# Sliding-window attention and a three-way maxout feed-forward on one core: the scores of tiles 6, 12 and 18 as one unit

## The chip, the cores and the metric

The kernel runs on one core of a Trainium2 chip. The core has five instruction streams that run side by side and wait for each other by semaphores: TensorE (PE in the profile; its weight loads are listed apart as PEld), VectorE (DVE), ScalarE (ACT), GpSimd (POOL) and SyncE (SP), which here only issues DMAs. Matrix products are written to PSUM, which the program treats as eight banks of 512 float32 for each of 128 partitions. The metric is the time on the device in microseconds (us) for one launch; a lower time is better. In the profile, "the span" runs from the first to the last instruction, so the time of a run is a little longer than its span.

## The reference

Four batches of eight heads, 768 positions, head width 64. Each position attends to the 96 latest positions including itself and to the first eight positions of its sequence, with a bias that falls linearly with distance at a slope of its own for each head. The result, 3072 rows of 512, goes through a feed-forward layer with three weight matrices, whose elementwise maximum is projected back to 512.

```python
scores = scale * np.matmul(q, k.transpose(0, 1, 3, 2))
is_global = pos[None, :] < int(n_global)            # n_global = 8
is_local = (rel >= 0) & (rel < int(n_local))        # n_local = 96
bias = -slopes[:, None, None] * dist[None, :, :]
a = softmax(where(keep, scores + bias, -1e9)); attn = a @ v
x = attn.transpose(0, 2, 1, 3).reshape(B * S, H * D)
h = np.maximum(np.maximum(x @ w1, x @ w2), x @ w3)  # 512 -> 768
out = h @ w_out                                     # 768 -> 512
```

## The kernel before, in words

**Tiles.** The 3072 rows are 24 tiles of 128 positions. Six tiles make a batch, so tiles 0, 6, 12 and 18 begin a batch. Because the window is 96 long, a tile's queries need only the keys of the tile itself and of the tile before it; the eight global keys and values are copied into rows of the tile before (units G and V). A tile that begins a batch has no tile before it, and so half the scores of any other tile.

**A schedule written out by hand.** The string SCHEDULE holds 782 short codes. Each code calls one function, which issues the instructions of one piece of work, and the order of the codes is the order of the instructions on every engine; nothing reorders them afterwards. A code such as S7.1.0@2 reads: unit S, tile 7, group 1, variant 0, buffer slot 2. Slots are assigned by hand too: "@" gives the PSUM bank or the place in a ring of SBUF buffers, and a unit that takes a bank has to wait until the bank's last reader is done. Units S and A take two neighbouring banks, units F, O, t and x one bank.

**The units that matter here.**

- l, c, x, y, X: load q and k, cast them to bf16 (c), and bring them into transposed form, either by TensorE (x, line 274) and a copy (y, line 285), or by one DMA transpose on SP's queue (X, line 290).
- S (line 347): the scores of a tile for four heads (group 0 or 1), eight small matmuls for an ordinary tile, four for a tile that begins a batch. The pairs of heads alternate between the two banks of the unit. The result is 128 partitions by 4 heads by 2 key tiles by 128 queries; in a tile that begins a batch only one of the two key places is filled.
- e (line 354): the exponential on ScalarE, from PSUM to a buffer P in SBUF; 1024 elements per partition for an ordinary tile, 512 for a tile that begins a batch.
- m (lines 363 and 365): the product of P with the mask and bias factors (wmask), on VectorE; line 363 for ordinary tiles, 365 for tiles that begin a batch.
- A (lines 389 and 392): probabilities times values, with a column of ones in the values for the sum; 16 matmuls for an ordinary tile, 8 for a tile that begins a batch, into two banks.
- n (lines 400 and 401): reciprocal of the sum and scaling, from PSUM to xb on VectorE; t, u (lines 416 and 419) or Z (line 422, DMA) transpose xb into xT for the feed-forward.
- F (line 431): one 128-row block of one of the three products of a chunk of 2 or 4 tiles, four matmuls into one bank. f evicts it: the first of the three by a cast to h01 (line 445, on ScalarE with variant 0, on VectorE with variant 1), the second by a maximum with h01 (447), the third by a maximum into ht (450).
- O (line 455) and o (line 469): the output projection of one tile, six matmuls into one bank, and its copy to the staging buffer, on ScalarE (variant 0) or VectorE (variant 1). s sends it out.
- G and V (lines 313 and 323): the copies of global keys and values.

**Where the change sits.** Three stretches: around tile 6 (about 45 to 56 us in the profile), where tile 8's transposes x4 and y4 and the feed-forward blocks F1.4 and F1.5 share the banks with S6, S7, A6 and A7; around tile 12 (about 64 to 72 us); and around tile 18 (about 90 to 100 us), whose keys and queries come by the DMA transpose X18. TensorE takes its instructions strictly in the order of the schedule, so a unit that waits holds everything behind it.

Of the kernel before, what the change touches and what calls it, by code (L numbers as in the profile page):

```python
# [55 lines left out]
    F3.0.0@1 f3.4.0.0@4 f3.0.0.1@0 m13.0.1 v13.1.1 f2.4.2.1 F3.1.0@4 F3.3.0@5 c0.9.2.0@2 f3.3.0.0@1 c1.7.2.0
    A12@2 n12@1 f2.3.2.1 f3.1.0.1@2 F3.1.1@1 f3.1.1.1 v13.0.1 l1.9.2@0 c1.9.2.0 F3.0.2@0 F3.0.1@5 f3.0.1.1
    F3.1.2@4 f3.0.2.1@1 F3.2.0@1 F3.2.2@2 f3.1.2.1 F3.5.0@3 A13@4 V13.1.1 f3.5.0.1@3 n13@0 l2.9.2@2 l0.8.2@5
    c0.8.2.2@0 v19.0.2 V13.0.0 f3.2.0.0@0 v14.0.2 F3.5.1@0 F3.2.1@6 f3.2.1.1 f3.2.2.1 F3.3.1@1 F3.5.2@3 v18.1.0
    X14@3 v14.1.2 X15 f3.5.1.1 f3.3.1.1 F3.4.1@2 c1.8.2.0 S14.0.0@4 S14.1.0@0 e14.0@6 G14.2 f3.4.1.1 F3.4.2@6  # L60
# [4 lines left out]
    G16.0 Z14 o3.1.0@11 m16.0.1 V15.0.1 S17.0.0@0 Z12 S19.0.0@2 Z15 l2.8.2@1 e19.0@7 S17.1.0@4 e17.1@0 m17.1.1  # L65
    F4.4.0@6 e17.0@5 l0.11.2@1 s1.0 l2.10.2@0 F4.2.0@7 l1.10.2@2 F4.1.0@2 F4.5.0@3 v16.0.0 v16.1.0 F4.3.0@0
    A16@4 f4.2.0.0@2 Z18@2 V16.1.2 V16.0.2 f4.3.0.0@0 G18.0 F4.1.2@1 f4.1.0.1@3 m17.0.1 v17.0.1 v17.1.1
    l2.11.2@2 n16@3 s3.1 f4.5.0.0@4 m19.0.1 l0.10.2@3 F4.0.1@0 F4.1.1@7 m19.1.1 f4.4.0.0@1 F4.5.2@6 A19@2
    V19.0.2 v20.0.2 c0.11.2.2@1 c0.10.2.2@2 Z16 n19@1 Z19 G19.0 s0.1 s2.1 f4.1.1.1 f4.1.2.1@0 V19.1.1 F4.0.0@4
    F4.4.1@5 A17@2 c1.10.2.0 f4.0.0.1@3 n17@2 F4.5.1@7 f4.5.1.1 F4.2.1@1 F4.3.2@4 f4.5.2.1 f4.4.1.1 F4.0.2@2  # L70
# [25 lines left out]
def kernel(  # L96
# [239 lines left out]
    def u_S(slot, T, g, how):  # L336
        n = 2 if T % NT else 1
        biased[T, g] = how
        if not how:
            sps[T, g] = ring("sp", slot, [128, 2, 2, 2, 128], FP32, "sp")  # L340
        sp = sps[T, g]
        for ds in range(n):
            for j2 in range(2):
                jp = 2 * g + j2
                for hh in range(2):
                    hsl = slice(64 * hh, 64 * hh + 64)
                    nc.tensor.matmul(sp[:, hh, j2, ds], qT(T - ds, 1, hsl, jp), qT(T, 0, hsl, jp),  # L347
                                     start=not how, stop=True, skip_group_check=True)
# [8 lines left out]
    def u_m(slot, T, g, how):  # L357
# [4 lines left out]
        if T % NT:  # L362
# [15 lines left out]
    def u_A(slot, T):  # L378
# [3 lines left out]
        for g in range(2):  # L382
            P = Pt[T, g]
            for j2 in range(2):
                for hh in range(2):
# [3 lines left out]
                    nc.tensor.matmul(o, P[:, i, 0], heads(va(T))[:, h], start=True, stop=(t == 0),  # L389
# [220 lines left out]
```

## Time and profile before

| What | Value |
|---|---|
| Time, median of 3 runs (lowest to highest) | 175.57 us (175.31 to 175.96) |
| Time of the profiled execution | 175.37 us |
| Its span | 173.6 us |
| TensorE busy | 165.8 us, 95% of the span |
| VectorE busy | 130.5 us, 75% |
| ScalarE busy | 97.5 us, 56% |
| GpSimd busy | 52.7 us, 30% |
| Granted TensorE clock | 1.00 |

The profile's page gives busy times by engine and by group of instructions, and the chain of work that ended last: starting from the last instruction, it goes back at each step to whatever released that instruction, or to the one before it on its engine. The window table gives busy time by stretch, and the timeline lists instructions in order of time, with the idle time ahead of them in brackets and what ended it. In a timeline row the second number is the time from the start of the first to the end of the last instruction that is merged into the row; neighbouring matmuls overlap, so the chain, which counts each piece from the end of the one before, is the better view of how long a run of matmuls took.

### The profile page before, as it was taken

What the parts mean: (1) busy time and instruction counts of PE and PEld (TensorE: products, weight loads), DVE (VectorE), ACT (ScalarE), POOL (GpSimd) and SP (SyncE); (2) the same over time, 40 slices, a digit from 0 to 9 for tenths busy, and PEclk for the clock granted to TensorE, in tenths of its full rate; (3) what the DMA queues carried; (4) which work ended last, traced back from release to release, by engine and by line L of the source; (5) the groups of instructions that cost most, each with busy time, mean ns of one, the idle gap of its engine ahead of it and who ended that gap; (6) DMA issues with size and microseconds to landing.
All of it is one profiled execution on the core that took longest, in us unless ns stands there. A gap on an engine that the chain in (4) does not pass through costs nothing.

```text
span 173.6 us, 3857 instructions
## 1 busy us (share of the span) xinstructions
PE 165.8 (95%) x1485; PEld 93.7 (54%) x1507; DVE 130.5 (75%) x267; ACT 97.5 (56%) x149; POOL 52.7 (30%) x97
## 2 busy tenths in 40 slices
PE   7998999999999999999999999999999999999992
PEld 2455745567676767744445545544445654444442
DVE  7889884988699799798798479599578994064910
ACT  5988896771876878653657689200345551502032
POOL 4049396059498315200630001440530000000000
PEclk9999999999999999999999999999999999999999
DMA  5999999999999899699978799999990044380026
GB/s 135 359 294 324 401 362 384 291 364 315 291 292 189 130 263 166 175 299 289 148 129 138 72 212 312 309 228 265 262 203 29 0 125 119 124 302 0 2 73 233
DMA packets 66259, 37.36 MB, mean 215 GB/s; under 512 B 24128, under 2 KB 61120, under 8 KB 66240
## 3 DMA queue, kind: packets, MB, share of 16 engines
q1 hardware_dynamic: 66096, 37.04, 84.6%
q8 instruction: 12, 0.20, 0.5%
q10 hardware_dynamic: 144, 0.07, 0.1%
q14 instruction: 7, 0.06, 0.1%
HBM read 25.17 MB, written 6.29 MB: 181 GB/s over the span
## 4 chain that ended last, share of the span: by engine, by line
PE 85%; DVE 5%; DMA 3%; ACT 3%; issue 2%; SPq 0%; DVEq 0%
PE psum L431 51%; PE psum L455 18%; PE psum L347 6%; PE psum L389 3%; DMA rawqk<-in_k_dram 3%; PE psum L392 3%; PE psum L274 2%; ACT P L354 1%; PE psum L268 1%; PE psum L333 1%; PE psum L416 1%; DVE xb L401 1%; ACT xT L419 1%; ACT qb L193 1%; DVE P L365 0%
## 5 line engine op out<-in xcount | busy, mean ns | idle before, releaser
L431 PE MATMUL psum<-xT,w 128*128 128x512 bf16 (+1 forms) x491 | 97.4, 348 | 1.3 <-DVE ht L450 0.3
L431 PEld LDWEIGHTS <-w 128*128 128x128 bf16 x504 | 47.7, 98 | 42.4 <-issue 0.7
L354 ACT ACTIVATE P<-psum 128x1024 bf16<-128x1024 f32 (+1 forms) x48 | 43.3, 955 | 10.6 <-PE psum L347 10.5
L447 DVE TENSOR_TENSOR h<-h,psum 128x512 bf16<-128x512 bf16 (+1 forms) x42 | 25.1, 606 | 16.0 <-PE psum L431 12.1
L455 PE MATMUL psum<-wo,ht 128*128 128x512 bf16 (+2 forms) x147 | 33.5, 362 | 0.5
L445 ACT CAST h<-psum 128x512 bf16<-128x512 f32 (+1 forms) x27 | 13.9, 525 | 31.0 <-PE psum L431 27.8
L450 DVE TENSOR_TENSOR ht<-h,psum 128x512 bf16<-128x512 bf16 (+1 forms) x42 | 26.2, 643 | 2.1 <-PE psum L431 1.0
L363 DVE TENSOR_TENSOR P<-P,wmask 128x1024 bf16<-128x1024 bf16 x34 | 24.6, 738 | 1.6 <-ACT P L354 1.5
L455 PEld LDWEIGHTS <-ht 128*128 128x128 bf16 x156 | 13.9, 98 | 13.5
L252 POOL CAST va<-rawv 64x512 bf16<-64x512 f32 x28 | 18.4, 662 | 4.0 <-DMA rawv<-in_v_dram 2.9
L321 POOL COPY va<-vaf 4x260 int32<-4x260 int32 x17 | 6.8, 400 | 40.9 <-PE psum L392 40.5
L401 DVE TENSOR_TENSOR xb<-psum,rz 128x512 bf16<-128x512 f32 x24 | 16.6, 692 | 0.8
L469 ACT COPY staging<-psum 128x512 f32<-128x512 f32 x14 | 8.2, 592 | 12.8 <-PE psum L455 12.8
L347 PE MATMUL psum<-qkT 64*128 64x128 bf16 x352 | 14.5, 217 | 0.7 <-DVE qkT L313 0.4
L347 PEld LDWEIGHTS <-qkT 64*128 64x128 bf16 x352 | 10.1, 94 | 8.2 <-issue 6.2
L389 PEld LDWEIGHTS <-P 128*128 128x128 bf16 x192 | 12.6, 97 | 3.2 <-ACT P L354 0.4
L199 POOL CAST qb<-rawq 128x512 bf16<-128x512 f32 x14 | 9.1, 678 | 16.6 <-DMA rawq<-in_q_dram 16.4
L389 PE MATMUL psum<-va,P 128*128 128x65 bf16 x160 | 12.6, 193 | 0.1
L445 DVE CAST h<-psum 128x512 bf16<-128x512 f32 (+1 forms) x15 | 9.1, 614 | 4.0 <-PE psum L431 3.9
L392 PEld LDWEIGHTS <-P 128*128 128x128 bf16 x160 | 10.4, 97 | 1.5 <-DVE va L323 0.3
L199 POOL CAST qb<-rawk 128x512 bf16<-128x512 f32 x10 | 6.4, 677 | 12.5 <-DMA rawk<-in_k_dram 12.3
L392 PE MATMUL psum<-va,P 128*128 128x65 bf16 x128 | 9.9, 193 | 0.0
(72 smaller groups left out, 121.1 us busy)
## 6 DMA issues: line engine op xcount, KB each, us to landing
rawv<-in_v_dram SPq DMA_DIRECT2D x12, 512.0 KB, 7.1
out_dram<-staging SPq DMA_DIRECT2D x22, 256.0 KB, 2.5
rawq<-in_q_dram SPq DMA_DIRECT2D x10, 512.0 KB, 7.0
rawk<-in_k_dram SPq DMA_DIRECT2D x10, 512.0 KB, 7.4
staging<-in_moe_w_dram SPq DMA_DIRECT2D x3, 1024.0 KB, 9.3
staging<-in_moe_w_dram SPq DMA_DIRECT2D x3, 512.0 KB, 8.8
staging<-in_moe_w_out_dram SPq DMA_DIRECT2D x3, 512.0 KB, 6.4
rawqq<-in_q_dram SPq DMA_DIRECT2D x1, 512.0 KB, 4.2
```

The source lines that it names most:

```text
L252: copies[how](heads(va(T))[64 * e:64 * e + 64, :, 0:D], src)
L347: nc.tensor.matmul(sp[:, hh, j2, ds], qT(T - ds, 1, hsl, jp), qT(T, 0, hsl, jp), start=not how, stop=True, skip_group_check=True)
L354: nc.scalar.activation(P[:, :, 0:n], sps[T, g].rearrange("p a b d n -> p (a b) d n")[:, :, 0:n], AF.Exp, bias=0.0, scale=scale)
L363: mul(P, P, wmask[:, g, :, 0:2])
L389: nc.tensor.matmul(o, P[:, i, 0], heads(va(T))[:, h], start=True, stop=(t == 0), skip_group_check=True)
L392: nc.tensor.matmul(o, P[:, i, 1], heads(va(T - 1))[:, h], start=False, stop=True, skip_group_check=True)
L401: nc.vector.tensor_tensor(out=x.rearrange("p (g h) d -> p g h d", g=2), in0=o4[:, :, :, 0:64], in1=rz[:, :, :, None].to_broadcast([128, 2, ...
L431: nc.tensor.matmul(ps, w123[f // 2][:, j, dm, (f % 2) * 128:(f % 2) * 128 + 128], xT[c][:, dm], start=(dm == 0), stop=(dm == 3))
L445: copies[how](h01, ps)
L447: nc.vector.tensor_max(h01s[c, f], h01s[c, f], ps)
L450: nc.vector.tensor_max(dst, h01s[c, f].rearrange("p (t e i) -> p t e i", e=2, i=64), ps.rearrange("p (t e i) -> p t e i", e=2, i=64))
L455: nc.tensor.matmul(po, ht[c][:, f, tt * 128:(tt + 1) * 128], wo[:, f, cols], start=(f == 0), stop=(f == NF - 1))
```

## The change

For tiles 6, 12 and 18 the two S units become one (group 2): its eight matmuls write head group 0 into the first key place and head group 1 into the second, in one pair of banks. One exponential of 1024 elements and one mask product of 1024 elements follow, where there were two of 512 each; A reads head group g from place g. Tile 12's single unit stands where S12.1 stood, in the same banks; tile 18's stands right behind S15.1, in banks 4 and 5, ahead of O2.0, A14 and O2.1, where S18.0 and S18.1 stood behind O2.1 in banks 0 to 3. X18 comes earlier in the string but keeps its place on SP's queue. Around tile 6 the order and the slots change: S7.1 goes to banks 4 and 5, F1.4.1, O0.2 and F1.5.0 to banks 2, 3 and 1; F1.4.2 and x4.0 come before A7, and O0.3 before F1.1.2; n7 comes before f1.4.2; V7.0 (ScalarE) comes behind the exponentials of tile 8. Two evictions move from VectorE to ScalarE: f1.5.0 (256 elements) and o0.1 (512 elements).

The schedule, cut to the lines that hold the changed units:

```diff
-    f1.1.0.0@3 y3.0.2.0 S6.0.0@0 S6.1.0@4 G6.2 c1.4.2.2@1 c0.4.2.2 l0.5.2@0 c0.5.2.2@2 f1.1.1.1 f1.4.0.0@1
-    e6.0@4 S7.0.0@6 S7.1.0@2 l1.5.2@6 c1.5.2.2 e6.1@5 c1.6.2.2@0 e7.1@6 F1.4.1@0 e7.0@7 l2.4.2@1 O0.2@1 f1.4.1.1
-    m7.1.1 x4.1.2@0 F1.5.2@2 F1.5.0@3 m7.0.1 v8.1.2 F1.5.1@4 A7@6 f1.5.0.1@0 f1.5.1.1 m6.1.1 m6.0.1 o0.2.0@0
-    y4.1.2.0@0 f1.5.2.1 x4.0.2@3 y4.0.2.0 G7.0 l0.6.2@1 c0.6.2.2 F1.4.2@5 O0.1@4 f1.4.2.1 n7@2 o0.1.1@1 A6@0
-    l2.5.2@2 S8.1.0@2 S8.0.0@6 n6@3 V7.1.1 G8.1 v8.0.2 F1.1.2@4 O0.3@5 t6@0 v11.0.2 v9.0.2 v9.1.2 f1.1.2.1
-    V7.0.0 t7@1 e8.1@0 e8.0@3 S9.0.0@2 u6.0@2 S9.1.0@6 m8.1.1 u7.1 o0.3.0@2 O0.0@4 e9.1@1 m8.0.1 o0.0.0@3 e9.0@2
+    f1.1.0.0@3 y3.0.2.0 S6.2.0@0 G6.2 c1.4.2.2@1 c0.4.2.2 l0.5.2@0 c0.5.2.2@2 f1.1.1.1 f1.4.0.0@1 e6.2@4
+    S7.0.0@6 S7.1.0@4 l1.5.2@6 c1.5.2.2 c1.6.2.2@0 e7.1@6 F1.4.1@2 e7.0@7 l2.4.2@1 O0.2@3 m6.2.1 f1.4.1.1 m7.1.1
+    x4.1.2@0 F1.5.2@2 F1.5.0@1 m7.0.1 v8.1.2 F1.5.1@4 F1.4.2@5 o0.2.0@0 f1.5.0.0@0 y4.1.2.0@0 x4.0.2@3 A7@6
+    f1.5.1.1 f1.5.2.1 n7@2 f1.4.2.1 O0.1@4 y4.0.2.0 G7.0 l0.6.2@1 c0.6.2.2 o0.1.0@1 A6@0 l2.5.2@2 S8.1.0@2
+    S8.0.0@6 n6@3 V7.1.1 G8.1 v8.0.2 O0.3@5 F1.1.2@4 t6@0 v11.0.2 v9.0.2 v9.1.2 f1.1.2.1 t7@1 e8.1@0 e8.0@3
+    V7.0.0 S9.0.0@2 u6.0@2 S9.1.0@6 m8.1.1 u7.1 o0.3.0@2 O0.0@4 e9.1@1 m8.0.1 o0.0.0@3 e9.0@2 F2.4.0@5 m9.1.1
...
-    F2.4.1@7 A9@4 V9.1.2 V9.0.2 X13 O1.0@6 l2.7.2@0 n9@0 S12.0.0@0 f2.4.1.1 m10.0.1 l2.6.2@1
-    v15.1.2 v12.1.2 F2.5.2@0 O1.1@1 v12.0.2 S12.1.0@2 e12.1@3 S13.1.0@4 m11.0.1 Z9 f2.5.2.1 S13.0.0@6 o1.1.1@5
+    S12.2.0@2 e12.2@3 S13.1.0@4 m11.0.1 Z9 f2.5.2.1 S13.0.0@6 o1.1.1@5 F2.4.2@0 A11@2 n11@2 F2.0.1@1 e13.1@1
...
-    f3.5.2.1 F3.3.2@7 e14.1@7 f3.4.2.1 m14.0.1 m14.1.1 v19.1.2 v15.0.2 S15.0.0@0 e15.0@0 S15.1.0@2 G15.1 e15.1@5
-    f3.3.2.1 O2.0@6 A14@0 V14.1.2 o2.0.1@6 n14@3 X18@0 O2.1@7 v18.0.0 o2.1.0@7 m15.0.1 S18.0.0@0 S18.1.0@2 X19
-    Z13@1 V14.0.1 O3.3@6 m15.1.1 e18.0@3 e18.1@4 X16@1 o3.3.0@8 A15@0 n15@2 O3.0@7 S19.1.0@0 m18.0.1 S16.1.0@2
-    m18.1.1 e19.1@1 S16.0.0@4 O3.2@6 o3.0.1@9 e16.0@2 V15.1.2 A18@0 e16.1@6 n18@0 o3.2.1@10 m16.1.1 X17 O3.1@7
+    m14.1.1 v19.1.2 v15.0.2 S15.0.0@0 e15.0@0 S15.1.0@2 S18.2.0@4 G15.1 e15.1@5 e18.2@3 v18.0.0 f3.3.2.1 O2.0@6
+    A14@0 V14.1.2 o2.0.1@6 n14@3 O2.1@7 o2.1.0@7 m15.0.1 X19 Z13@1 m15.1.1 V14.0.1 O3.3@6 X16@1 o3.3.0@8 A15@0
+    n15@2 O3.0@7 S19.1.0@0 S16.1.0@2 m18.2.1 e19.1@1 S16.0.0@4 O3.2@6 o3.0.1@9 e16.0@2 V15.1.2 A18@0 e16.1@6
```

The functions:

```diff
 def u_S(slot, T, g, how):
+        if g == 2:
+            for half in range(2):
+                for j2 in range(2):
+                    for hh in range(2):
+                        hsl = slice(64 * hh, 64 * hh + 64)
+                        nc.tensor.matmul(sp[:, hh, j2, half], qT(T, 1, hsl, 2 * half + j2), qT(T, 0, hsl, 2 * half + j2),
+                                         start=True, stop=True, skip_group_check=True)
+            return
 def u_e(slot, T, g):
-        n = 2 if T % NT else 1
+        n = 2 if T % NT or g == 2 else 1
 def u_m(slot, T, g, how):
-        if T % NT:
+        if g == 2:
+            mul(P, P, wmask[:, :, :, 2].rearrange("p g i n -> p i g n"))
+        elif T % NT:
 def u_A(slot, T):
-            P = Pt[T, g]
+            P, first = (Pt[T, 2], g) if (T, 2) in Pt else (Pt[T, g], 0)
-                    nc.tensor.matmul(o, P[:, i, 0], heads(va(T))[:, h], start=True, stop=(t == 0),
+                    nc.tensor.matmul(o, P[:, i, first], heads(va(T))[:, h], start=True, stop=(t == 0),
```

More of the change, by code (lines that the diff above doesn't have):

```diff
@@ L56 @@
[L56 to L60, printed above, removed]
@@ L66 @@
[L66 to L70, printed above, removed]
@@ new lines @@
+    f2.4.0.0@2 A8@0 V8.0.2 n8@1 F2.5.0@4 F2.2.1@6 f2.5.0.1@4 F2.1.0@7 f2.1.0.0@0 G9.0 F2.5.1@5 V8.1.2 F2.2.0@4
+    f2.5.1.1 m9.0.1 f2.2.0.0@1 X10@1 X11 S10.1.0@0 f2.2.1.1 e10.1@6 S10.0.0@2 e10.0@7 v10.0.1 X12@2 G10.1 G12.1
+    F2.4.1@7 A9@4 V9.1.2 V9.0.2 X13 O1.0@6 l2.7.2@0 n9@0 f2.4.1.1 m10.0.1 l2.6.2@1 v10.1.1 S11.1.0@2 S11.0.0@4
+    e11.1@5 F2.2.2@7 f2.2.2.1@0 F2.3.0@0 F2.1.1@1 F2.0.0@7 f2.3.0.0@3 m10.1.1 e11.0@0 f2.0.0.0@1 A10@2 V10.0.2
+    f2.1.1.1 m11.1.1 o1.0.0@4 n10@3 Z8@0 V10.1.0 l0.7.2@2 v11.1.2 v15.1.2 v12.1.2 F2.5.2@0 O1.1@1 v12.0.2
@@ new lines @@
+    A13@4 V13.1.1 f3.5.0.1@3 n13@0 l2.9.2@2 l0.8.2@5 c0.8.2.2@0 v19.0.2 V13.0.0 f3.2.0.0@0 v14.0.2 F3.5.1@0
+    F3.2.1@6 f3.2.1.1 f3.2.2.1 F3.3.1@1 F3.5.2@3 v18.1.0 X14@3 v14.1.2 X15 X18@0 f3.5.1.1 f3.3.1.1 F3.4.1@2
+    c1.8.2.0 S14.0.0@4 S14.1.0@0 e14.0@6 G14.2 f3.4.1.1 F3.4.2@6 f3.5.2.1 F3.3.2@7 e14.1@7 f3.4.2.1 m14.0.1
+    m14.1.1 v19.1.2 v15.0.2 S15.0.0@0 e15.0@0 S15.1.0@2 S18.2.0@4 G15.1 e15.1@5 e18.2@3 v18.0.0 f3.3.2.1 O2.0@6
+    A14@0 V14.1.2 o2.0.1@6 n14@3 O2.1@7 o2.1.0@7 m15.0.1 X19 Z13@1 m15.1.1 V14.0.1 O3.3@6 X16@1 o3.3.0@8 A15@0
@@ new lines @@
+    m23.1.1 Z21@0 V21.1.1 m23.0.1 V21.0.2 A22@4 V22.0.2 V22.1.1 n22@1 s3.2 Z20 o4.1.0@4 O4.3@1 A23@6 O4.2@3 Z22
+    o4.3.0@11 f5.5.2.1 O5.2@0 O5.3@1 n23@2 O5.1@4 o5.3.0@1 Z23 F6.4.2@1 o4.0.1@7 F6.0.0@2 F6.0.2@5 F6.0.1@6
+    o5.2.0@5 F6.1.2@0 o5.1.0@3 F6.4.0@4 F6.2.0@7 f6.0.0.0@2 f6.0.1.1 F6.4.1@2 f6.0.2.1@0 F6.3.1@5 o4.2.0@6
+    f6.2.0.1@3 F6.3.0@3 f6.4.0.1@0 F6.1.1@4 f6.4.1.1 f6.4.2.1 s4.3 s4.0 f6.3.0.0@4 F6.3.2@1 F6.1.0@2 s5.2
+    F6.2.1@3 s4.2 s5.1 s4.1 f6.1.0.0@1 s3.0 s5.3.2 f6.3.1.1 f6.1.1.1 f6.3.2.1 f6.2.1.1 F6.2.2@2 f6.2.2.1
```

41 lines of the change are left out of this document (19 added, 22 removed).

## The prediction

> **What bounds the kernel now.** First the page: busy times and the chain that ended last.
>
> ```profile
> PE 165.8 (95%) x1485; PEld 93.7 (54%) x1507; DVE 130.5 (75%) x267; ACT 97.5 (56%) x149; POOL 52.7 (30%) x97
> PE 85%; DVE 5%; DMA 3%; ACT 3%; issue 2%; SPq 0%; DVEq 0%
> ```
>
> TensorE is the bound: 95% busy, 85% of the chain. The change takes no matmul away. What it saves on ScalarE and VectorE counts only where TensorE now waits for them, so the waits of TensorE and the window table come next:
>
> ```profile
> PE psum L431 <- DVE ht L450: 0.3, 1, 0.3
> ```
>
> ```profile
> 45.00:50.00 5.00, 4.99 (x69) 3.67 (x69) 3.34 (x6) 4.33 (x7) 2.69 (x5) 1.00 1.15 294
> 50.00:55.00 5.00, 4.61 (x58) 3.17 (x56) 4.87 (x12) 3.59 (x5) 4.60 (x9) 1.00 1.25 240
> 65.00:70.00 5.00, 4.95 (x71) 3.76 (x70) 4.39 (x10) 4.36 (x8) 2.78 (x5) 1.00 1.20 171
> 90.00:95.00 5.00, 4.95 (x56) 2.70 (x57) 4.72 (x11) 3.54 (x7) 0.40 (x1) 1.00 0.71 117
> ```
>
> Columns behind the stretch: its length, then busy PE, PEld, DVE, ACT, POOL. By this table TensorE has 0.39 us of idle time in 50 to 55 us (tile 6) and next to none by tiles 12 and 18. The 0.3 us wait lies at 86.8 us, which nothing in the change touches. But overlapping matmuls hide waits in a busy figure, so the chain in order of time is the third view. Columns: start, length, what.
>
> ```profile
> 45.04 0.96 PE psum L347 x24
> ...
> 49.66 0.14 PE psum L389
> ...
> 50.25 0.45 PE psum L274 x8
> 50.69 0.44 PE psum L431 x4
> ...
> 52.42 0.26 PE psum L389 x8
> 52.68 0.35 PE psum L347 x8
> 53.03 0.67 DVE staging L469
> ...
> 53.75 0.60 PE psum L431 x4
> 54.34 1.29 PE psum L455 x6
> 55.64 0.45 PE psum L416 x8
> 61.14 0.55 PE psum L347 x16
> 97.49 0.78 PE psum L347 x24
> ```
>
> Three losses stand there (S, A, F, O are lines 347, 389 with 392, 431 and 455). The 24 score matmuls of S6 and S7 take 0.96 us, against 0.78 for as many at 97.49: 0.18 lost, where S7.1 in banks 2 and 3 waits for VectorE's f1.1.1. A7 runs from 49.66 to 50.25, 0.59 us, against 0.49 for A14 (92.20 to 92.69, quoted below): 0.10 lost to the mask m7.0. From the start of S8 at 52.68 to F1.1.2 at 53.75 are 1.07 us for 16 score matmuls that take 0.55 elsewhere: 0.52 lost. S8.0 waits for n7 to leave banks 6 and 7, and F1.1.2 waits for o0.1, 0.67 us on VectorE, to leave bank 4. In all 0.80 us.
>
> TensorE's busy row would put the loss at 0.39. The Trainium skill, "Perfetto Trace Analysis", section "Identifying the Most-Contended Engine", says that matmul busy time is a poor measure because matmuls are pipelined; the trace agrees, with 4.99 of 5.00 busy in a stretch whose chain shows 0.28 lost. By the busy row the sum below would be -0.39 + 0.30, or 175.5; by the chain it is 175.1.
>
> **The change, part by part.** Durations by form:
>
> ```profile
> L354 ACT ACTIVATE P<-psum 128x1024 bf16<-128x1024 f32 x40 | 39.1, 1026 | 8.7 <-PE psum L347 8.7
> L354 ACT ACTIVATE P<-psum 128x512 bf16<-128x512 f32 x8 | 4.6, 598 | 1.9 <-PE psum L347 1.8
> L363 DVE TENSOR_TENSOR P<-P,wmask 128x1024 bf16<-128x1024 bf16 x34 | 24.6, 738 | 1.6 <-ACT P L354 1.5
> L365 DVE TENSOR_TENSOR P<-P,wmask 128x512 bf16<-128x512 bf16 x7 | 3.6, 542 | 0.2 <-ACT P L354 0.2
> L445 ACT CAST h<-psum 128x256 bf16<-128x256 f32 x8 | 2.9, 374 | 5.2 <-PE psum L431 5.2
> L445 DVE CAST h<-psum 128x256 bf16<-128x256 f32 x4 | 1.7, 418 | 0.0
> L469 ACT COPY staging<-psum 128x512 f32<-128x512 f32 x14 | 8.2, 592 | 12.8 <-PE psum L455 12.8
> L469 DVE COPY staging<-psum 128x512 f32<-128x512 f32 x6 | 4.1, 682 | 0.2 <-PE psum L455 0.2
> ```
>
> Merging saves ScalarE 2 x 0.598 - 1.026 = 0.17 us and VectorE 2 x 0.542 - 0.738 = 0.35 us per tile, three times; the rehomed evictions take 0.42 + 0.68 = 1.10 us from VectorE and give 0.97 to ScalarE. None of it is TensorE time, so by itself it is worth nothing. The mask product's wmask operand is strided anew, and no row shows that form. A floor is its present 0.74; a ceiling is two products of 512, 1.08. I take 0.74, since 1024 elements is the nearer row. At 1.08 the m6 and f1.4.1 behind it would be done at about 48.1, still ahead of F1.5.2 at 48.2.
>
> *Tile 6.* I walk the queues again from 45.04 with the lengths above. S7.1 in banks 4 and 5 no longer waits for f1.1.1: scores 0.82 (0.78 and a small start), then F1.4.1 0.60, O0.2 1.29, x4.1 0.45, three F blocks of 0.44, F1.4.2 0.44 and x4.0 0.45 bring A7 to 50.41. m7.0 ends now at 49.5 (row below), and m6 ahead of it costs at most a tenth, so A7's wait is gone; its cover is now F1.4.2 and x4.0.
>
> ```profile
> 48.44 1.09 DVE L363 TENSOR_TENSOR P<-P,wmask 128x1024 bf16<-128x1024 bf16 x1
> ```
>
>  A7 0.46, O0.1 1.29, A6 0.26 put S8 at 52.42, 0.26 earlier than now. n7 now follows f1.5.1 and f1.5.2 (0.4 each from F1.5.1's end at 49.7), starts when A7 is done at about 51.1 and ends at 52.0; S8.0 comes at 52.7, without a wait. S8's other source is ScalarE: o0.2 from 48.4, f1.5.0 at 49.3 (once F1.5.0 is through), y4.1 and y4.0 of 1.0 each, G7 0.2, done at 51.9, 0.5 us ahead of S8. That queue is what gets late next: everything that the change gives ScalarE here stands ahead of S8.
>
> ```profile
> 50.73 1.01 ACT L285 COPY qkT<-psum 128x1024 bf16<-128x1024 bf16 x1 [1.05 <-PE psum L274]
> 51.64 0.22 ACT L313 COPY qkT<-kg 128x32 bf16<-128x32 bf16 x1
> 51.76 0.62 ACT L323 COPY va<-vaf 4x520 bf16<-4x520 bf16 x1
> ```
>
> The 1.05 us of idle time in the first row is the slack that f1.5.0 uses up. o0.1 on ScalarE is free at 52.3, done at 52.9; F1.1.2 waits for it only at 54.3, behind O0.3, and O0.3 waits for f1.4.2 on VectorE, done at 52.4 against 53.0. V7.0, 0.62 us, now behind e8.0, is wanted by A8 some 2 us later. So t6 starts at 54.8 where it started at 55.64: a gain of 0.80, with the ends 0.39 (busy row) and 0.84 (the walk).
>
> *Tile 12.* TensorE has no idle time here, so 4 score matmuls moved from 64 to 68.7 us cost and save nothing. The exponential is a new wait. Now e12.1, of 512, and A11 behind it in the same banks 2 and 3 stand thus:
>
> ```profile
> 69.01 1.51 ACT L354 ACTIVATE P<-psum 128x512 bf16<-128x512 f32 x2 [0.61 <-PE psum L347]
> ...
> 69.35 0.61 PE L431 MATMUL psum<-xT,w 128*128 128x256 bf16 x4
> 69.79 0.19 PE L389 MATMUL psum<-va,P 128*128 128x65 bf16 x1
> ```
>
> e12.1 started at 69.01 with ScalarE idle for 0.61 us before it, and was done near 69.6; A11 started at 69.79. The merged unit starts 0.11 earlier and is 0.14 longer on TensorE, so e12.2 starts at about 69.05, takes 1.03, and lets go of banks 2 and 3 at 70.1. A11, S13 and F2.4.2 having gone by, would start at 69.79: a wait of 0.3, and all that follows on TensorE, F2.0.1 first, waits with it. Its ends are 0.14 (counting from 69.96, where the chain has F2.4.2 end) and 0.45 (e12.2 late by one small eviction). e11 gains what e12.0 no longer takes ahead of it, and A11 has no use for that.
>
> *Tile 18.* Again no idle time on TensorE, so the move gains nothing. S18 comes ahead of O2.0 (1.40 behind score matmuls), A14 (0.49) and O2.1 (1.29), 3.2 us earlier.
>
> ```profile
> 92.20 0.03 PE psum L389
> ...
> 92.69 0.86 PE psum L455 x4
> ...
> 93.98 0.33 PE psum L347 x8
> ...
> L290 SPq DMA_TRANSPOSE qkT<-qb x2: 1430/1734/2037, 81.6 to 83.1; - x2
> DMA to landing us min/median/max: 5.8/5.9/6.1
> ```
>
> X18, issued at 83.1 and landing 6.1 us later at 89.2, covered S18 at 93.98 by 4.8 us; at 90.8 it covers it by 1.6, and by 1.1 once TensorE runs 0.5 us ahead. On VectorE m15.1 and V14.0 follow o2.0, n14 and m15.0, all 0.33 later behind the later O2.0: done near 95.5, A15 at 95.7. Both covers are thin, and both count as nothing.
>
> *Sum.* -0.80 + 0.30 + 0 = -0.50 us on the profiled execution's 175.37, or 174.87. That execution is 0.20 below the median of 175.57, so I predict 175.1 for the median.
>
> **Rivals.**
> *The gain is not there, or is taken back.* If A11 waits 0.45 and tile 6 gives only the busy row's 0.39, or DMA landings that don't move take the rest, the time is 175.57 + 0.06 = 175.6. For it: VectorE and POOL are 4.87 and 4.60 of 5.00 busy in 50 to 55. Against it: the evictions that TensorE waited for leave VectorE.
> *A11 doesn't wait.* Should F2.4.2 and S13 hide e12.2, the whole 0.80 stays: 174.8. Against it: e12.2's end at 70.1 by the rows.
> *Slower: S18 waits for X18.* TensorE stands at S18, with O2.0, A14 and O2.1 behind it, until the transpose lands. The landing would have to slip by 1.1 us to cost anything, by 1.6 us to use up the gain and by 2.5 us for 0.5% more than before; at 3 us it gives 177.0. For it: X14, X15, X18 and X19 follow each other on SP, the longest landing of their line is 6.1 us, and it is X18's own. Against it: the transposes' loads are fed by the same queues as before, and landings of this line spread over 2.5 us (next row), not beyond.
>
> ```profile
> DMA to landing us min/median/max: 3.6/4.6/6.1
> ```
>
> That row is the view of line 290's fourteen transposes. The Trainium skill, "Perfetto Trace Analysis", section "DMA Instruction — HWDGE (DVE, Sync)", says that the profile's DMA row shows the issue and not the movement of data; the trace agrees, X18's issue being over in about 2 us and its landing 6.1 us after its start.
>
> **How the numbers follow.** Forecast 0.54 (own range 174.8 to 175.4), gain lost 0.20, no wait at A11 0.15, S18 or another new wait slower 0.11. Measured medians lie within about 0.2 us of their middle, and 0.5% of 175.57 is 0.88 us, about what a measurement tells from no change: faster is under 174.7, slower over 176.45. The forecast of 175.1 is thus "same". Half of the no-wait case and a fifth of the forecast's lower tail fall under 174.7: faster 0.18. Slower takes the last case and a little of the lost gain: 0.13. Same 0.69. The range goes from 174.5 (0.84 and a low median) to 176.1 (part of the slower cases).
>
> **What would show it.** Right: in the chain, the 24 score matmuls at 45 us take about 0.8, A7 follows x4.0 without a wait, no VectorE piece stands between S8 and t6, and t6 starts near 54.8; A11 waiting 0.2 to 0.4 us for the exponential near 69 us; S18 directly behind S15 with no gap. Wrong: TensorE waiting for y4.0 or G7 ahead of S8, for the DMA transpose at S18, for V14.0 ahead of A15, or A11 without a wait.

## Result and profile after

The kernel after the change takes 174.56 us (median of 7 runs, 174.29 to 174.87), the kernel before, run beside it, 175.41 us (7 runs, 175.09 to 175.96). The ratio is 0.9945, its 95% interval 0.9926 to 0.9963. The forecast of 175.1 was a change of -0.27%; it is twice that, -0.55%. The profiled execution took 174.52 us with a span of 172.7 us, against 175.37 and 173.6.

In after, x is line 273 and V line 322, one lower than in before; from S on the line numbers are seven to nine higher: line 346 is the merged S, 354 the ordinary S, 361 e, 370 the merged m, 398 and 401 A, 440 F, 464 O, 425 t. Busy times and the chain's shares on the page of after:

```profile
PE 165.3 (96%) x1485; PEld 93.2 (54%) x1507; DVE 129.0 (75%) x262; ACT 98.2 (57%) x148; POOL 52.4 (30%) x97
PE 83%; DMA 6%; DVE 4%; ACT 3%; issue 2%; SPq 0%
```

The number of matmuls is the same. DVE fell by 1.5 us and ACT rose by 0.7, and neither says where the span became shorter. A part of the chain, 3% before and 6% now, is a transfer. The windows of after, with the columns of the table shown before:

```profile
50.00:55.00 5.00, 4.95 (x68) 3.31 (x66) 3.22 (x9) 4.31 (x8) 4.25 (x9) 1.00 1.39 267
65.00:70.00 5.00, 4.82 (x78) 3.45 (x77) 3.61 (x9) 4.25 (x7) 3.28 (x5) 1.00 1.20 275
```

In 50 to 55 us TensorE went from 4.61 to 4.95 busy with 10 more matmuls; in 65 to 70 it lost 0.13. The chain of after in order of time (start, length, what):

```profile
44.98 0.33 PE psum L346 x8
45.31 0.45 PE psum L354 x16
...
49.79 0.45 PE psum L273 x8
...
50.72 0.22 PE psum L464
50.98 1.03 PE psum L464 x4
52.01 0.26 PE psum L398 x8
52.27 0.55 PE psum L354 x16
52.82 1.40 PE psum L464 x6
54.22 0.44 PE psum L440 x4
54.66 0.45 PE psum L425 x8
...
67.45 4.81 DMA xT<-xb
72.30 0.39 PE psum L440
...
82.72 4.37 PE psum L440 x20
87.08 0.55 PE psum L354 x16
...
89.47 0.60 PE psum L354 x16
90.07 0.22 PE psum L346 x8
90.29 1.40 PE psum L464 x6
...
94.80 0.12 PE psum L401
```

*Tile 6.* S6 and S7 take 0.78 us (0.33 + 0.45). A7 fills the 0.48 from 50.24 to 50.72. No VectorE piece is left between S8 at 52.27 and t6, which starts at 54.66 where it started at 55.64.

*Tile 18.* S18's eight matmuls follow S15 without a gap and take 0.22 us, where they took 0.33 before.

*New.* F3.4.0 is released at 72.3 us by the transpose Z10, which took 4.81 us to land. *Gone.* The VectorE pieces that ended at 86.8 us before, ahead of F3.4.1 and S14, are no longer there: TensorE's blocks run through from 82.72 to 87.08.

A difference between two executions need not be one between two programs. So the table cuts TensorE's timeline of every profiled run at fixed first matmuls; each column is the time from one to the next, in us, and what a column holds is in its head.

| Run | S6 to t6 (tile 6) | t6 to t11 (tile 12, A11) | t11 to A12 (Z10) | A12 to A13 | A13 to S14 | S15 to S19 (tile 18) | span |
|---|---|---|---|---|---|---|---|
| before | 10.49 | 16.12 | 4.55 | 6.30 | 5.31 | 7.24 | 173.6 |
| after | 9.59 | 16.42 | 4.85 | 6.30 | 4.95 | 7.12 | 172.7 |
| e1 tile 6 alone | 9.59 | 16.11 | 5.40 | 6.30 | 5.30 | 7.24 | 173.3 |
| e2 tile 12 alone | 10.20 | 16.42 | 4.55 | 6.30 | 5.16 | 7.25 | 173.4 |
| e3 tile 18 alone | 10.63 | 16.11 | 4.55 | 6.41 | 5.32 | 7.12 | 173.8 |
| e4 without tile 12 | 9.58 | 17.16 | 4.55 | 6.38 | 4.95 | 7.12 | 173.2 |
| e5 evictions back | 9.59 | 16.41 | 4.55 | 6.30 | 5.27 | 7.12 | 172.9 |
| e6 merge of tile 6 alone | 10.39 | 16.11 | 5.13 | 6.30 | 5.33 | 7.25 | 173.9 |
| e7 S12.2 early | 9.58 | 16.40 | 4.55 | 6.36 | 4.94 | 7.12 | 172.6 |
| e8 before, four fewer | 10.25 | 16.11 | 4.55 | 6.30 | 5.22 | 7.24 | 173.2 |
| e9 merged S18, old place | 9.59 | 16.42 | 4.55 | 6.30 | 5.03 | 7.37 | 173.0 |
| e10 after, four more | 9.59 | 17.66 | 4.59 | 6.30 | 4.94 | 7.12 | 173.7 |
| e11 V13.1 on GpSimd | 9.58 | 16.42 | 4.79 | 6.30 | 4.95 | 7.12 | 172.8 |
| e12 = e4 and e11 | 9.59 | 16.11 | 4.55 | 6.30 | 4.95 | 7.12 | 172.2 |
| e13 before again | 10.51 | 16.11 | 4.55 | 7.49 | 5.31 | 7.24 | 175.2 |
| e14 before, four more | 10.44 | 16.11 | 4.55 | 7.28 | 4.94 | 7.24 | 174.1 |
| e15 before, V13.1 on GpSimd | 9.86 | 16.11 | 5.29 | 6.30 | 4.94 | 7.25 | 173.4 |
| e16 after again | 9.59 | 16.42 | 4.55 | 6.30 | 5.12 | 7.13 | 173.0 |

The column of tile 18 follows the program, and so does that of tile 12, but for a late transfer in e4 and a late cast in e10. Tile 6 takes 9.58 or 9.59 us in all ten profiles with the new order. With the old order (before, e2, e3, e8, e13, e14, e15) it takes 9.86 to 10.63, with a mean of 10.34, although the code there is the same in all seven. The columns of Z10, A12 to A13 and A13 to S14 change between executions of one program. Of the 90 runs of the kernel before, 62 lie within 0.4 us of the median of their group and the others up to 1.4 us away, so effects of 0.1 to 0.3 us are read from these stretches and not from the times.

In the old order, tile 6's stretch is long where VectorE's mask products of tile 6 are long (m6.1 and m6.0, line 365; n7 and then o0.1 follow them on VectorE). Here they stand with GpSimd's casts, first in before, then in e15, the fastest of the seven:

```profile
49.13 2.94 POOL L199 CAST qb<-rawk 128x512 bf16<-128x512 f32 x4
50.31 1.28 DVE L365 TENSOR_TENSOR P<-P,wmask 128x512 bf16<-128x512 bf16 x2
```

```profile
49.98 0.75 DVE L365 TENSOR_TENSOR P<-P,wmask 128x512 bf16<-128x512 bf16 x2
50.56 2.32 POOL L199 CAST qb<-rawk 128x512 bf16<-128x512 f32 x4 [0.67 <-DMA rawk<-in_k_dram]
```

In e15 the casts of k begin only as the second product ends, and the two take 0.75 us together; in the other six, casts run before and beside them, and the products take 1.16 us (e2, tile 6 in 10.20) to 1.59 (e3, 10.63). The casts begin when a load has landed. In the new order the merged product runs at about 46.5 us and took 0.69 us in nine of the ten profiles (0.78 in e1), and m7.0 may take 0.69 us or 1.09 (e7) without A7 starting later. By these rows the new order takes away a dependence on the landing of loads, and what it saves is 0.27 to 1.04 us, by the execution. No run isolates the casts' part by an edit.

### The profile page after: what moved, and what is told of

Same layout as the page of the kernel before. It is cut to its first block, busy times and chain, and to the rows that moved or that the text cites. A ratio compares the mean times of both kernels' runs of the same rounds, so it can differ in the third digit from the quotient of the medians.

```text
span 172.7 us, 3845 instructions
## 1 busy us (share of the span) xinstructions
PE 165.3 (96%) x1485; PEld 93.2 (54%) x1507; DVE 129.0 (75%) x262; ACT 98.2 (57%) x148; POOL 52.4 (30%) x97
## 4 chain that ended last, share of the span: by engine, by line
PE 83%; DMA 6%; DVE 4%; ACT 3%; issue 2%; SPq 0%
PE psum L440 51%; PE psum L464 17%; PE psum L354 5%; DMA rawqk<-in_k_dram 3%; DMA xT<-xb 3%; PE psum L398 3%; PE psum L401 2%; PE psum L273 2%; ACT P L361 1%; PE psum L267 1%; DVE P L372 1%; PE psum L332 1%; PE psum L425 1%; ACT xT L428 1%; ACT qb L192 1%
## 5 line engine op out<-in xcount | busy, mean ns | idle before, releaser
L251 POOL CAST va<-rawv 64x512 bf16<-64x512 f32 x28 | 19.0, 685 | 4.5 <-DMA rawv<-in_v_dram 3.5
L478 ACT COPY staging<-psum 128x512 f32<-128x512 f32 x15 | 8.7, 590 | 13.3 <-PE psum L464 13.3
L354 PE MATMUL psum<-qkT 64*128 64x128 bf16 x328 | 13.3, 217 | 0.6 <-DVE qkT L312 0.4
L354 PEld LDWEIGHTS <-qkT 64*128 64x128 bf16 x328 | 9.4, 94 | 6.7 <-issue 4.7
L409 DVE RECIPROCAL rz<-psum 128x8 f32<-128x8 f32 x24 | 4.8, 202 | 6.6 <-PE psum L401 4.5
```

What stands on the lines that cost most here:

```text
L251: copies[how](heads(va(T))[64 * e:64 * e + 64, :, 0:D], src)
```

## The experiments

The kernel before ran beside each group: medians 175.48 us (23 runs) for e1 to e4, 175.66 (35) for e5 to e8, 175.65 (25) for e9 to e12, and one run of 175.36 for e13 to e16, which were one execution each. The ratios are those of the record; they differ from the quotients of the medians by up to 0.2%.

### The three parts, each alone: e1, e2, e3, and without tile 12: e4

e1 is the kernel before with the changed lines around tile 6 (S6.2 to V7.0, the two evictions with them). Here and below, codes that stay are left out:

```diff
-S6.0.0@0 S6.1.0@4 e6.0@4 S7.1.0@2 e6.1@5 F1.4.1@0 O0.2@1
+S6.2.0@0 e6.2@4 S7.1.0@4 F1.4.1@2 O0.2@3 m6.2.1
...
-A7@6 f1.5.0.1@0 F1.4.2@5 O0.1@4 o0.1.1@1 F1.1.2@4 O0.3@5
+F1.4.2@5 f1.5.0.0@0 A7@6 O0.1@4 o0.1.0@1 O0.3@5 F1.1.2@4
```

> The changed order, slots, merged unit and moved evictions of tile 6 only; tiles 12 and 18 as before. Theory (the three stretches add up; tile 6 carries the gain, the wait of A11 costs 0.2 to 0.3 us, tile 18 gains about 0.13 us): 0.9 us faster than before, t6 starting near 54.7, no wait of A11 on the exponential. Rival (the gain behind tile 6 is held at F3.4.0 by the DMA transpose Z10, so what A11 waits costs nothing): 0.4 to 0.6 us faster, with a DMA piece of line 431 ahead of F3.4.0 in the chain near 72 us.

Measured: 174.86 us, ratio 0.9944 (0.9922 to 0.9966). S6 to t6 is 9.59, as in after, with all else of tile 6's stretch as there. By its ratio, tile 6 carries the gain. In its one profile, though, t11 to A12 is 5.40 us, 0.85 more than the 4.55 of most runs, as the recorded rival had it: TensorE arrives earlier and stands for Z10. This row of its weight loads shows it (waited for: total, times, longest):

```profile
PEld L440 <- DMA xT<-xb: 1.0, 1, 1.0
```

e2 is the kernel before with tile 12's unit merged:

```diff
-S12.0.0@0
...
-S12.1.0@2 e12.1@3
+S12.2.0@2 e12.2@3
```

> Tile 12's merged unit only; tiles 6 and 18 as before. Theory: A11 waits for the exponential e12.2, 0.2 to 0.3 us slower than before. Rival (a later wait takes the loss in, as the VectorE wait ahead of F3.4.1 at 86.8 us or the landing of Z10): within 0.1 us of before.

Measured: 175.35 us, ratio 0.9989 (0.9973 to 1.0006). t6 to t11 is 16.42 against 16.11 or 16.12 in all runs without the merge but e4: 0.30 us longer. The waits of the weight loads between 60 and 72 us in after name the cause, and e2 has the same row; no run with tile 12 unmerged has it:

```profile
PEld L398 <- ACT P L361: 0.4, 1, 0.4
```

That is A11 behind e12.2: in after e12.2 ends at 69.06 us and A11 starts at 69.12. The time shows no loss, against the theory and as the recorded rival had it. The interval, -0.47 to +0.11 us of 175.48, does not hold +0.30. In e2's one profile the +0.30 stands beside -0.29 at tile 6 and -0.15 ahead of S14, which the merge does not touch; what takes the loss in over its twelve runs is not shown.

e3 is the kernel before with tile 18's unit merged and moved:

```diff
-S15.1.0@2 G15.1
+S15.1.0@2 S18.2.0@4 G15.1 e15.1@5 e18.2@3
...
-S18.0.0@0 S18.1.0@2 e18.0@3 e18.1@4
```

> Tile 18's merged unit behind S15.1 only; tiles 6 and 12 as before. Theory (score matmuls set beside other score matmuls save a switch on TensorE): 0.1 to 0.2 us faster than before, S18's eight matmuls 0.22 us in the chain instead of 0.33, and the projection behind A14 1.29 instead of 1.40. Rival (A15 waits for V14.0 and gives it back): no change.

Measured: 175.29 us, ratio 0.9990 (0.9974 to 1.0006). S15 to S19 is 7.12 as in after, 0.12 less than in before. No wait for X18 appears.

e4 is the kernel after with tile 12's units as before:

```diff
+S12.0.0@0 e12.0@4
-S12.2.0@2 e12.2@3
+S12.1.0@2 e12.1@3 m12.0.1 m12.1.1
```

> The changed kernel with tile 12 in two units as before. Theory (A11's wait counts): 0.2 to 0.3 us faster than the changed kernel, 1.1 to 1.2 us faster than before. Rival (F3.4.0 is held by the landing of Z10 either way): as the changed kernel, 0.85 us faster than before, with a longer DMA piece ahead of F3.4.0.

Measured: 174.48 us, ratio 0.9933 (0.9916 to 0.9950). A11 no longer waits, but in the profiled execution TensorE stood 1.1 us in the same stretch:

```profile
PEld L353 <- DMA qkT<-qb: 0.6, 1, 0.6
63.11 0.17 DVE L309 COPY kg<-qkT 128x32 bf16<-128x32 bf16 x1 [1.57 <-DMA qkT<-qb]
```

S12.0's operands, transposed by X12, landed at 63.09 us, against 59.95 in e12. S12.0 lost 0.15 us to that, and VectorE's G12 (the second row) was held too, with n9 behind it, which reads the banks that S11.0 takes, so that S11.0 stood another 0.5 us. e12 has the same codes there and takes 16.11 without that hold. The gain of 0.3 from leaving tile 12 alone is thus seen in e12's stretch; by the times e4 and after cannot be told apart.

### What in tile 6 carries the gain: e5, e6

e5 is the kernel after with the two evictions back on VectorE:

```diff
-f1.5.0.0@0
+f1.5.0.1@0
...
-o0.1.0@1
+o0.1.1@1
```

> The changed kernel with f1.5.0 and o0.1 evicted on VectorE again, all else as changed. Theory (tile 6's gain comes from the order and the slots, above all O0.3 set ahead of F1.1.2, so that o0.1 has 1.4 us more; the engine matters less): within 0.2 us of the changed kernel, t6 starting near 54.8. Rival (the moved evictions carry the gain, since VectorE was the late one): 0.4 to 0.5 us slower than the changed kernel, t6 near 55.2.

Measured: 174.70 us, ratio 0.9962 (0.9938 to 0.9986). The chain of e5, where line 424 is t6:

```profile
54.30 0.44 PE psum L439 x4
54.74 0.45 PE psum L424 x8
```

S6 to t6 is 9.59 and F1.1.2 directly precedes t6, as in after. In this profile the rehomed evictions gain nothing. What is left to remove the waits is the order and the slots: O0.3 now comes ahead of F1.1.2, which o0.1 thus holds no longer even on VectorE, and n7 ahead of f1.4.2.

e6 is the kernel before with tile 6's unit merged in place; order, slots and evictions stay:

```diff
-S6.0.0@0 S6.1.0@4 e6.0@4 e6.1@5 m6.1.1 m6.0.1
+S6.2.0@0 e6.2@4 m6.2.1
```

> The kernel before with tile 6's scores, exponential and mask merged in place, in banks 0 and 1, with the order, slots and evictions of before. Theory (merging by itself frees no TensorE time; F1.4.1 in bank 0 now waits for an exponential of 1024 instead of 512): no gain on t6, or up to 0.3 us later, from 55.64; time as before plus 0 to 0.3, less the VectorE pause of 0.3 us at 85 us, if that goes with the number of VectorE instructions. Rival (less work on VectorE and ScalarE is the gain): t6 0.3 us or more earlier than 55.64.

Measured: 175.21 us, ratio 0.9978 (0.9958 to 0.9999). Its chain:

```profile
45.38 1.03 ACT P L361
46.45 0.60 PE psum L440 x4
...
55.43 0.45 PE psum L425 x8
```

The merge alone makes a new wait of 0.5 us, F1.4.1 in bank 0 behind e6.2, and S6 to t6 is 10.39, inside the 9.86 to 10.63 of the old order. The order and the slots carry the gain of tile 6, with the merge to which they are fitted; which of the moves counts for how much was not tried. The time is 0.2% below before, with an interval that just leaves out 1.

### Tile 12's unit elsewhere: e7

e7 is the kernel after with S12.2 where S12.0 stood, in banks 0 and 1:

```diff
-S12.2.0@2 e12.2@3
...
-n9@0
+n9@0 S12.2.0@0
...
-v10.1.1
+v10.1.1 e12.2@4
```

> The changed kernel with tile 12's merged unit where S12.0 stood before (banks 0 and 1, ahead of S11), so that A11's banks are free early. Theory (A11's wait is real, and the landing of Z10 hid it in the one profile): A11 doesn't wait, 0.2 us faster than the changed kernel. Rival (Z10's landing holds F3.4.0 in every run): as the changed kernel, with the wait on the DMA longer by what A11 doesn't wait.

Measured: 175.09 us, ratio 0.9989 (0.9963 to 1.0014), with single runs up to 176.46. t6 to t11 stays at 16.40: up to S13 it is 13.61 against after's 13.33, and from there 2.79 against 3.09, since A11 waits no longer. The loss of 0.3 has only moved ahead of S13. It stands at F2.3.0, the first unit in bank 0 behind S12.2: it starts 0.74 us behind F2.2.2, against 0.45 in after, at 64.61 us, right behind e12.2, which ends at 64.56. It is the same exponential that is met earlier.

### Merging or neighbourhood at tile 18: e9

e9 is the kernel after with the merged S18 at the old place behind O2.1:

```diff
-S15.1.0@2 S18.2.0@4
+S15.1.0@2
...
+S18.2.0@0 e18.2@3
```

> The changed kernel with tile 18's merged unit at its old place, behind O2.1 in banks 0 and 1, instead of behind S15.1. Theory (what tile 18 gains, 0.12 us between S15 and S19, comes from setting score matmuls beside score matmuls, so that TensorE changes its kind of matmul once less): 7.24 us from S15 to S19 as before. Rival (it comes from the merged exponential and mask): 7.12 us as in the changed kernel. The time can't tell 0.12 us.

Measured: 174.63 us, ratio 0.9942 (0.9926 to 0.9957); S15 to S19 is 7.37, the longest of all. Its chain, lines 345 (S18), 353 (S) and 463 (O):

```profile
89.40 0.60 PE psum L353 x16
90.00 1.40 PE psum L463 x6
...
91.88 1.29 PE psum L463 x6
93.18 0.33 PE psum L345 x8
93.51 1.40 PE psum L463 x6
94.91 0.15 PE psum L397
```

Alone, S18 takes 0.33 and the projection behind it 1.40; behind S15, as in after, S18 takes 0.22, and the projection that followed it finds 1.29. So 0.11 us are lost on each change between score matmuls, which use 64 rows of the array (64*128 in the timeline), and the others with 128, and the move saves one pair, 0.22; A15's wait for V14.0 gives a part back. In e9 A15's first piece takes 0.15 instead of 0.03, which makes the stretch 0.12 longer than in before: A15 takes banks 0 and 1, which the merged exponential e18.2 reads until 94.73 us, 0.11 ahead of A15's first weight load. That it is this wait is argued from the slots. The neighbourhood is the gain, not the merging. The Trainium skill, "TensorEngine Tiling (Array Packing)", section "Key Properties", says that changing the tiling mode drains TensorE; the trace agrees in that each change costs 0.11 us, but no row names a drain.

### The wait ahead of S14: e8, e10, e11, e13 to e16, and the best parts together: e12

The largest difference outside tile 6, 5.31 to 4.95 from A13 to S14, lies where the change touches nothing. In before VectorE stood idle for 0.30 us ahead of f3.2.1, with no releaser. In before's timeline stand V13.1, GpSimd's cast of q (load l0.8) and f3.2.1:

```profile
83.16 0.29 DVE L323 COPY va<-vaf 4x520 bf16<-4x520 bf16 x1 [1.27 <-PE psum L392]
83.41 1.17 POOL L199 CAST qb<-rawq 128x512 bf16<-128x512 f32 x2 [12.90 <-DMA rawq<-in_q_dram]
85.29 0.69 DVE L447 TENSOR_TENSOR h<-h,psum 128x512 bf16<-128x512 bf16 x1 [0.30 <-issue]
```

A first theory tied the pause to the number of VectorE instructions ahead of it (the change removes four; f3.2.1 is the 159th in before and in e3, the 155th in after). e8 takes four away from before, e10 adds four to after, e14 four to before:

```diff
-        for tvar in va_first + va_ring:
-            nc.vector.memset(heads(tvar)[:, :, 64:65], 1.0)
+        for n, tvar in enumerate(va_first + va_ring):
+            (nc.vector if n < 4 else nc.gpsimd).memset(heads(tvar)[:, :, 64:65], 1.0)
```

> The kernel before with four of the eight small fills of the ones columns at the start moved from VectorE to GpSimd: the schedule is untouched, VectorE executes four instructions fewer ahead of everything else. Theory (the 0.30 us pause of VectorE ahead of f3.2.1 near 85 us, put down to nothing in the profile, is tied to the count of VectorE instructions; the changed kernel moved it away from the path): pause gone, F3.4.1 with no wait or one of under 0.1 us, 0.25 to 0.35 us faster than before. Rival (the pause comes from something else that tile 6 or 12 changed): pause still there, time as before.

```diff
+        for n in range(4):
+            nc.vector.memset(heads(va_ring[5])[:, :, 64:65], 1.0)
```

> The changed kernel with four more small fills on VectorE at the start (of a ones column that is filled already), so that VectorE's count of instructions is again that of the kernel before up to tile 13. Theory (VectorE's 0.30 us pause is tied to its count of instructions): the pause is back on f3.2.1 near 84.5 us, put down to nothing, if GpSimd's cast doesn't collide with V13.1 in this run, and from A13 to S14 it takes 5.3 us instead of 4.95. Rival (the pause belonged to tile 6 or 12 as they were): no pause, 4.95 us.

> The kernel before with four more instructions on VectorE at its start (small memsets, 0.1 us each, long before anything waits). If the pause goes by the count of VectorE's instructions, it falls four instructions earlier, on the copy V13.1 or the cast ahead of it, or is gone, and f3.2.1 starts 2.48 us behind A13 if that place has slack. If it belongs to f3.2.1 itself or to its neighbours on other engines, it stays ahead of f3.2.1 and A13 to S14 is 5.31. If it is chance, either can come out.

Measured: e8 175.07 us, ratio 0.9966 (0.9939 to 0.9992); e10 174.60 us, 0.9948 (0.9928 to 0.9967); e14 175.88 us in one execution. There is no pause in any of the three. e10 has f3.2.1 in the 159th place again and still takes 4.94, so the count does not explain it. The 5.22 of e8 is another thing, the one that the next runs show.

e13 and e16 are the kernels before and after, unchanged.

> The kernel before, unchanged. If the 0.30 us pause of VectorE ahead of f3.2.1 belongs to the program: A13 to S14 takes 5.31 us again, with the same 0.30 us that no engine explains. If it belongs to the one execution: 4.95 us, or 5.2 to 5.3 us where GpSimd's cast of q (load l0.8) starts ahead of V13.1 and lengthens it from 0.29 to 0.5 to 0.7 us. S6 to t6 10.2 to 10.6, S15 to S19 7.24 in either case.

> The kernel after, unchanged. If its stretch A13 to S14 of 4.95 us belongs to the program, it comes again; if it hangs on when GpSimd's cast of q starts, it is 4.95 with the cast behind V13.1 and 5.0 to 5.3 with the cast ahead of it. If the wait for Z10 belongs to the program, t11 to A12 is 4.85 again; if it hangs on the spread of the transfers, it lies between 4.55 and 5.4. S6 to t6 9.59, t6 to t11 16.42, S15 to S19 7.12 in either case.

Measured: e13 176.99 us and e16 174.79 us, one execution each. The kernel before has no pause this time and takes 5.31 all the same; the kernel after takes 5.12. VectorE's and GpSimd's rows, first of e13, then of e16 (in the first profile of after V13.1 started 0.45 us ahead of the cast and took 0.29):

```profile
84.43 1.23 POOL L199 CAST qb<-rawq 128x512 bf16<-128x512 f32 x2 [13.72 <-DMA rawq<-in_q_dram]
84.56 0.63 DVE L323 COPY va<-vaf 4x520 bf16<-4x520 bf16 x1 [1.91 <-PE psum L392]
```

```profile
82.31 1.23 POOL L198 CAST qb<-rawq 128x512 bf16<-128x512 f32 x2 [12.82 <-DMA rawq<-in_q_dram]
82.57 0.50 DVE L322 COPY va<-vaf 4x520 bf16<-4x520 bf16 x1 [1.28 <-PE psum L401]
```

Where GpSimd's cast starts first, V13.1 takes 0.40 to 0.70 us (0.63 in e13, 0.50 in e16), and everything behind it on VectorE is late: in e13 it ends at 85.19 and in e16 at 83.07, both 0.76 us behind the start of the cast, and 0.75 to 0.76 us are it in e1, e2, e5, e6, e8 and e9 too. Where V13.1 starts first it takes 0.29. The cast's start is set by a load's landing. Both orders occur in both programs: cast first in e13 and e16, V13.1 first in before, e14 and after. The stretch without the pause and without the collision is 4.94 with before's schedule too (e14). So the 0.36 us between the first two profiles belongs to the executions and not to the change. What made the pause itself, seen in before and e3 only, stays open.

e11 puts V13.1 of after on GpSimd, e15 that of before:

```diff
-V13.1.1
+V13.1.2
```

> The changed kernel with V13.1, a copy of 4 rows, on GpSimd instead of VectorE. Theory (VectorE's queue behind A13 sets when F3.4.1 can start; in some executions GpSimd's cast, whose start follows the landing of a load, runs first and stretches V13.1 from 0.29 to 0.6 us): A13 to S14 4.95 us or less in every execution, time 0 to 0.2 us under the changed kernel's. Rival (the collision is too rare or too small): as the changed kernel.

> The kernel before with the copy V13.1 on GpSimd instead of VectorE. If VectorE's time in the 2.5 us behind A13 carries the wait at 86.8 us: A13 to S14 falls from 5.31 to 4.95 us, whatever the cause of VectorE's delay, as collisions with GpSimd's cast cannot lengthen a copy that VectorE does not do. If the pause ahead of f3.2.1 has a cause of its own, it stays with 0.3 us and A13 to S14 is 5.0 to 5.3 us.

Measured: e11 174.68 us, ratio 0.9948 (0.9930 to 0.9965); e15 175.14 us in one execution. The stretch is 4.95 and 4.94: with V13.1 gone from VectorE the collision cannot delay it, and f3.2.1 starts 2.48 us behind A13, no sooner than in after. There is 0.1 to 0.4 to be had where the collision happens (A13 to S14 takes 5.03 to 5.33 there) and nothing where it does not. e15 also has TensorE wait 0.74 us longer for Z10, in the order of before, so that wait is no creation of the change either.

e13 and e14 lost 1.2 and 1.0 us between A12 and A13. TensorE's waits in e13 and ScalarE's timeline there:

```profile
PE psum L431 <- ACT h L445: 1.0, 1, 1.0
```

```profile
77.94 1.04 ACT L193 CAST qb<-rawq 128x1024 bf16<-128x1024 f32 x1 [3.40 <-DMA rawq<-in_q_dram]
78.89 0.58 ACT L445 CAST h<-psum 128x512 bf16<-128x512 f32 x1
```

ScalarE stood 3.4 us for a load of q with an eviction behind it that TensorE needed. In the first profile of before the same cast began at 76.31 after 2.0 us, with no loss. e10's 17.66 is of this kind: A8 waits 1.1 us for GpSimd's cast of v.

e12 is e4 with V13.1 on GpSimd: every part that gained, and neither tile 12's wait nor the collision.

> The same with tile 12 in two units again, so that A11 waits for no merged exponential. Theory (A11's 0.3 us and the collision are both losses of the changed kernel): 0.2 to 0.4 us faster than the changed kernel, 1.1 to 1.3 us faster than before. Rival (DMA landings hold TensorE further on and take it back): as the changed kernel, with waits on DMA at F3.4.0 or S10.

Measured: 174.65 us, ratio 0.9943 (0.9921 to 0.9966), lowest 173.96; its profile has the shortest span, 172.2 us, and in every stretch the best value or one within 0.01 of it. But other executions of it took up to 176.16 us, with no profile to say why, and by the times it cannot be told from after. No version tried is shown to beat it.

## Why the prediction was right and wrong

**Tile 6, -0.80: the mechanism right, the size that of one execution.** after took 9.59 us from S6 to t6 in both its executions. The steps came as walked: scores 0.78 against 0.82, A7 0.48 against 0.46, S8 at 52.27 against 52.42 without a wait, t6 at 54.66 against 54.8. The strided mask product took 0.684 us (mean of three), less than the floor of 0.74; the 1.08 did not come. Against 10.49 and 10.51 in the kernel before's two profiles the saving is 0.90; against all seven profiles of the old order it is 0.27 to 1.04, on average 0.75; the busy row's 0.39, its lower end, lies inside that spread. The prediction took the waits of one execution for those of the program: the 1.09 us of m7.0, from which it read A7's loss, is 0.69 in e15, and of the 0.52 that it counted behind S8 next to nothing is there either. Of the two reasons that it gave for o0.1 no longer holding F1.1.2, the move to ScalarE and the place behind O0.3, e5 shows that the place does it alone.

**Tile 12, +0.30: right in place and cause; that it reaches the end is not shown.** A11 waits for e12.2 for 0.30 us in every profile with the merged unit in banks 2 and 3, so the rival without a wait is refuted there. But "all that follows on TensorE, F2.0.1 first, waits with it" was counted in full to the end of the program, and e2's runs allow at most +0.11. In e1 and e4, which have the new tile 6 and the old tile 12, TensorE stood 0.85 and 1.05 us for transposes that landed late; such waits take in what is lost or saved ahead of them. In e12, with the same two, there was none. This is the prediction's rival of landings that take the gain back, seen in single executions and not in the medians.

**Tile 18, 0: the step that failed.** "Again no idle time on TensorE, so the move gains nothing" looked for idle time, and the cost lay in the matmuls' own lengths: 0.33 for S18 and 1.40 for a projection behind scores, both in the rows shown, against 1.29 elsewhere. Measured -0.12. The covers held: X18 held nobody (the slow rival did not come), and A15's wait for V14.0, which counted as nothing, was 0.1 us.

**The sum.** As stretches, the three terms measure -0.75 on average (-0.90 against before's own two profiles), +0.30 and -0.12: together -0.57, or -0.72. The forecast had -0.50. The medians differ by 0.85, and the ratio's interval is -0.65 to -1.30 us of 175.41, so the change moved the way that was forecast and about twice as far. What is shown of the difference is tile 18's 0.12. The rest stays open between two readings: tile 6 saves more than 0.75 in a usual execution, or tile 12's loss does not reach the end, without which the stretches give -0.87.

**"The 0.3 us wait at 86.8 us, which nothing in the change touches."** The wait was gone in the first profile of after, and seen alone that reads as a step that failed by 0.36. e13, e14 and e16 show that it comes and goes in either kernel, so the sentence stands. The first profiles' difference closes only with it: -0.90 (tile 6) + 0.30 (A11) + 0.30 (Z10) - 0.36 (A13 to S14) - 0.12 (tile 18) = -0.78, with -0.07 ahead of S6 -0.85, the difference of the two profiled executions. The Z10 wait and the missing wait at 86.8 us, both of the execution, nearly cancel there. That the first profiles and the medians both differ by 0.85 is therefore partly luck.

**What stays open.** Whether the change shifts how often loads hold TensorE or GpSimd's cast collides can't be told from 18 single profiles. The large losses between A12 and A13 (e13 and e14) came in two of the eight profiles without the new order at tile 6 and in none of the ten with it, too few to decide.

## What to carry to other kernels

Before a saved wait is summed, look for what a neighbour costs: a run of small matmuls is cheaper behind others of its shape, and that stands in the lengths of the chain's pieces, not in any idle time. When a unit of work grows, ask who uses its PSUM banks next: merging alone made TensorE wait 0.5 us for the longer exponential at tile 6 (e6) and 0.3 at tile 12. And take more than one profile of each kernel, before a wait is summed as well as before a difference is believed: here tile 6's waits were 0.27 to 1.04 us with the same code, and elsewhere 0.3 to 1.2 us came and went with the landing of loads.

## What the hardware showed beyond the forecast

- TensorE loses 0.11 us at each change between 64-row score matmuls and 128-row ones (0.33 against 0.22 for S18, 1.40 against 1.29 for a projection).
- A copy of 4 partitions by 520 elements on VectorE takes 0.29 us, and 0.40 to 0.70 when a cast on GpSimd has started before it. The Trainium skill, "SBUF — State Buffer", section "Who interferes with whom", says that VectorE's copies in a two-port mode and GpSimd share a pair of ports and that whoever issues first holds it for its whole instruction; the trace agrees: V13.1 ends 0.75 to 0.76 us behind the cast's start whether it came 0.05 or 0.35 us after it, which is the length of one cast, 0.61, and 0.14 more, and in after and before it came first and was not lengthened. No row names the mode of the copy.
- Two mask products of 512 elements on VectorE took 0.75 us together in e15 and 1.16 to 1.59 in six executions in which GpSimd's casts ran before and beside them.
- In one kernel the same load of q released its cast at 76.31 us in one execution and at 77.94 in another, and cost TensorE 1.0 us in the second. Of the 1.6 us by which e13's span exceeds before's, 1.2 lie in that stretch.
- VectorE stood still for 0.30 us ahead of one instruction, with nothing in the trace to wait for, in 2 of 18 profiles. Neither the count of its instructions nor a second execution of the kernel brought it back.
